# DMA transposes for three more attention units, earlier q and k for unit 1, and hidden-layer blocks laid around the last attn x v of batch 0

## Chip, cores, metric

One core of one Trainium2 chip. The metric is the device time of one execution in microseconds (us). Before the change it is 378.53 us (median of 3 runs, 378.49 to 378.64).

## The reference, cut to what matters

```python
# q, k, v: (8 batches, 12 heads, 448, 64) fp32; w_in (768, 2048), w_out (2048, 768)
scores = matmul(q, k.T) / 8
attn   = maximum(scores, 0) ** 2 / 448
x      = matmul(attn, v)             # laid out as (8 * 448, 768)
h      = x @ w_in
out    = maximum(h, 0) ** 2 @ w_out
```

The kernel works in fp16 with fp32 accumulation. It cuts the attention of a batch into three units of four heads, and a unit into seven tiles. Unit 0 has tiles 0 to 6, unit 1 has 7 to 13, and so on; batch 0 is units 0 to 2, batch 1 is units 3 to 5. A score matmul needs q and k with the head dimension on partitions, so each unit's q and k must be transposed first.

## The kernel before

There are two ways to get a transposed unit. Units 0 to 5 go the PE way (PE is TensorE, the matmul engine): whole-row loads (`load16`), 28 PE transposes into PSUM (the program's pools with `space=PSUM`), two copies out of PSUM. Units from 6 on go the DMA way: loads in pieces of 64 elements (`load_qk`), then two DMA transposes issued by SyncE (SP). All loads cast fp32 to fp16 and are issued by GpSimd (POOL).

```python
def load16(n):                        # whole rows: 2 x 448 elements a partition
    ...
    nc.gpsimd.dma_start(out=tq, in_=heads(q, n))
    nc.gpsimd.dma_start(out=tk, in_=heads(k, n))

def load_qk(n):                       # pieces of 64 elements (128 B in fp16)
    for src, nm in ((q, "qs"), (k, "ks")):
        t = blk_p.tile([P, J, 2, D], FP16, name=nm, tag=nm)
        for hh in range(2):
            nc.gpsimd.dma_start(out=t[:, :, hh, :], in_=...)

def dma_transpose(n):
    ts = new_qkt()
    for t, src in zip(ts, blks.pop(n)):
        nc.sync.dma_start_transpose(out=t, in_=src.rearrange("p j h d -> p (j h d)"))
    qkt[n] = ts
...
load16(0)
...
load_v(0); load16(1); load_v(1); load16(2); load_v(2)      # POOL's first loads
...
for i in range(11):                   # stage 1: batch 0's attention, tiles 0 to 20
    visit([t for t in (2 * i, 2 * i + 1) if t < NB0], turn={1: 1, 4: 2, 10: 3}.get(i))
    ...                               # loads of w_in and of units 3 to 5 between
load_v(6); load_w2(...) x 4; load_qk(6); load_qk(7)
# stage 2, "h stage": x @ w_in of batch 0 (16 groups of 6 matmuls), with batch 1's
# attention tiles and the PE transposes of units 4 and 5 woven in as "events";
# then x @ w_in of batch 1, where unit 6 (tile 42) starts at group 24
events.append((T_H + (1 + i // 2) * T_G, lambda i=i: sums_w2(i)))   # DVE sums of w_out blocks
events.append((T_H + (8 + i) * T_G, lambda i=i: sums_w1(i)))        # DVE sums of w_in blocks
```

The program gives each engine its instructions in a fixed order, and the traces show each waiting at the head of its own (below, PE stands still for 7.72 us before one score, with matmuls behind it that then wait for nothing). A small emission model (`at_pe`, `at_ve`: estimated times of PE and VectorE, DVE) decides where deferred DVE work is put in DVE's order:

```python
def av_unit():  ...; at_pe[0] += 2.65 ...                 # one attn x v of a unit
def visit(...): ...; at_pe[0] += 0.19 + 0.38 * len(tiles)
def fill(until):                      # puts deferred DVE work that the model thinks fits
    for d in (due, due_g):
        while d and max(at_ve[0], at_pe[0], d[0][0]) + d[0][1] <= until:
            put(d)
```

## Time and profile before

| | before |
|---|---|
| time, us | 378.53 |
| PE busy | 363.5 us, 96% |
| h stage of batch 0 begins in earnest | 30.22 us |
| tile 42 (unit 6) first scored | 71.05 us |
| q and k of unit 6 transposed by DMA | 65.95 us |

From the page of the kernel before: busy time per engine; the granted clock of PE, the DMA engines' busy share and what they moved, in 40 slices of the span; and the chain of work that ended last. PEld is PE's loading of weights, which overlaps PE. In the rows PEclk and DMA each digit is a slice in tenths; 9 is 90% or more.

```profile
PE 363.5 (96%) x3600; PEld 231.3 (61%) x3600; DVE 278.6 (74%) x515; ACT 249.8 (66%) x373; POOL 107.1 (28%) x128
PEclk9999999999999999999999999999999999999998
DMA  8999999999999999789498997893132200002333
GB/s 120 197 204 205 205 203 177 124 171 134 121 139 187 134 114 139 90 95 82 96 112 134 184 178 68 83 110 63 38 97 69 76 26 2 2 0 65 94 96 84
PE 81%; ACT 6%; DVE 6%; issue 2%; DMA 2%; POOL 1%; POOLq 0%; ACTq 0%; DVEq 0%
```

PE bounds the whole, but from the second slice to the sixth the loads run flat at 197 to 205 GB/s as well. What PE did, by the timeline (start, length, engine, line, operation, what was written and read, count, and the idle time before with what ended it):

```profile
11.49 0.58 PE L222 MATMUL slot<-ident,k 128*64 128x128 f16 x14 [0.72 <-DMA k<-in_k_dram]
...
30.22 2.81 PE L420 MATMUL mm<-xt,w 128*128 128x448 f16 x14 [0.25 <-ACT xt L280]
...
71.05 0.57 PE L252 MATMUL slot<-qT,kT 64*64 64x448 f16 x8
```

The transposes of unit 1's k waited 0.72 us for the load; tile 42 at 71.05 us waited for nothing. The DMA transposes of unit 6, by SP's timeline:

```profile
59.98 1.31 SPq L119 DMA_TRANSPOSE qT<-qs  x1
61.55 1.23 SPq L119 DMA_TRANSPOSE kT<-ks  x1
```

They landed 5.0 and 4.4 us after issue (the view of the tiles qT and kT), at 65.0 and 65.95 us, 5 us before tile 42. The wait of PE for squared attention tiles, by the waits view (total, times, longest, in us), is this:

```profile
PE slot L317 <- DVE at L369: 0.5, 2, 0.4
```

### The profile page before, as it was taken

Reading aid. Unit: us, or ns where it says so; the run is one execution under the profiler, and the core shown is the slowest. Engines: PE = TensorE matmul, PEld = TensorE weight load, DVE = VectorE, ACT = ScalarE, POOL = GpSimd, SP = SyncE. Lnnn points to the kernel's source line nnn. Section 1 sums busy time; section 2 is a strip of 40 time slices with the busy share of each in tenths; the row PEclk is TensorE's granted clock in tenths of the full one; section 3 lists DMA queues with packets and bytes.
Section 4 is the critical chain, followed back from the end, with each engine's and each line's share of the span. In section 5 each row is a group of like instructions: output and inputs, shape, how many; then the busy total and the mean of one; then the engine's idle time right before and its main releaser. Section 6 shows DMA issues by size and latency. Waiting matters only on the chain.

```text
span 377.6 us, 8806 instructions
## 1 busy us (share of the span) xinstructions
PE 363.5 (96%) x3600; PEld 231.3 (61%) x3600; DVE 278.6 (74%) x515; ACT 249.8 (66%) x373; POOL 107.1 (28%) x128
## 2 busy tenths in 40 slices
PE   7889999999999999999999999999999999999994
PEld 3544444444455678785555577877555588985663
DVE  1796567997767689897965758989956688995542
ACT  2897996686677798775566578877766785532220
POOL 8545431944440444404042243150000000000001
PEclk9999999999999999999999999999999999999998
DMA  8999999999999999789498997893132200002333
GB/s 120 197 204 205 205 203 177 124 171 134 121 139 187 134 114 139 90 95 82 96 112 134 184 178 68 83 110 63 38 97 69 76 26 2 2 0 65 94 96 84
DMA packets 121160, 42.65 MB, mean 113 GB/s; under 512 B 100832, under 2 KB 117760, under 8 KB 121120
## 3 DMA queue, kind: packets, MB, share of 16 engines
q0 software_dynamic: 82912, 23.01, 59.9%
q1 hardware_dynamic: 38048, 18.98, 26.2%
q8 instruction: 28, 0.46, 0.5%
q10 hardware_dynamic: 160, 0.10, 0.1%
q14 instruction: 12, 0.10, 0.1%
HBM read 45.61 MB, written 11.01 MB: 150 GB/s over the span
## 4 chain that ended last, share of the span: by engine, by line
PE 81%; ACT 6%; DVE 6%; issue 2%; DMA 2%; POOL 1%; POOLq 0%; ACTq 0%; DVEq 0%
PE mm L729 33%; PE mm L550 23%; PE slot L252 9%; PE mm L420 9%; PE slot L317 7%; ACT at L256 4%; DVE at L369 2%; DMA k<-in_k_dram 2%; PE slot L222 1%; DVE g L491 1%; ACT m L486 1%; DVE xt L283 1%; DVE s L602 1%; DVE g L498 0%; ACT qT L214 0%
## 5 line engine op out<-in xcount | busy, mean ns | idle before, releaser
L256 ACT ACTIVATE at<-slot 128x896 f16<-128x896 f32 x168 | 146.2, 920 | 33.0 <-PE slot L252 33.0
L369 DVE TENSOR_TENSOR at<-at 128x896 f16<-128x896 f16 x168 | 99.7, 618 | 15.7 <-ACT at L256 14.5
L108 POOL DMA_DIRECT2D qs<-in_q_dram x36 | 35.4, 984 | 121.3 <-DMA qT<-qs 113.6
L729 PEld LDWEIGHTS <-s 128*128 128x128 f16 x440 | 41.7, 98 | 32.0 <-issue 4.3
L252 PE MATMUL slot<-qT,kT 64*64 64x448 f16 x756 | 58.1, 360 | 2.6 <-ACT at L256 1.2
L550 PEld LDWEIGHTS <-w 128*128 128x128 f16 x576 | 54.4, 98 | 5.9 <-issue 5.4
L550 PE MATMUL mm<-xt,w 128*128 128x224 f16 x432 | 48.6, 259 | 0.0
L729 PEld LDWEIGHTS <-g 128*128 128x128 f16 x336 | 31.5, 98 | 24.0 <-issue 5.0
L550 PEld LDWEIGHTS <-ws 128*128 128x128 f16 x432 | 40.2, 98 | 6.7 <-issue 6.7
L729 PE MATMUL mm<-b,g 128*128 128x384 f16 x224 | 40.7, 326 | 0.0
L420 PE MATMUL mm<-xt,w 128*128 128x448 f16 x192 | 39.6, 353 | 0.3 <-ACT xt L280 0.3
L729 PE MATMUL mm<-b,s 128*128 128x384 f16 x216 | 39.6, 326 | 0.1
L729 PE MATMUL mm<-t,s 128*128 128x384 f16 x224 | 39.5, 326 | 0.0
L636 DVE SCALAR_TENSOR_TENSOR osb<-mm,u 128x384 f32<-128x384 f32 (+1 forms) x30 | 16.2, 541 | 31.2 <-ACT u L631 23.0
L252 PEld LDWEIGHTS <-kT 64*64 64x64 f16 x756 | 19.9, 104 | 31.1 <-issue 25.7
L108 POOL DMA_DIRECT2D ks<-in_k_dram x36 | 35.0, 975 | 9.9 <-DMA b<-in_moe_w_out_dram 5.8
L631 ACT ACTIVATE u<-mm 128x384 f32<-128x384 f32 x28 | 13.7, 491 | 32.6 <-PE mm L729 31.4
L571 POOL DMA_DIRECT2D out_dram<-osb x2 | 1.1, 563 | 120.5 <-DVE osb L636 120.5
L550 PE MATMUL mm<-x,ws 128*128 128x224 f16 x288 | 34.4, 259 | 0.9 <-ACT m L486 0.9
L317 PE MATMUL slot<-at,vt 64*64 64x448 f16 x588 | 32.2, 350 | 0.6 <-DVE at L369 0.5
L498 DVE TENSOR_TENSOR g<-g 128x896 f16<-128x896 f16 x48 | 29.7, 619 | 1.1 <-ACT g L501 0.2
L420 PEld LDWEIGHTS <-w 128*128 128x128 f16 x192 | 17.3, 98 | 19.1 <-issue 4.8
(66 smaller groups left out, 400.2 us busy)
## 6 DMA issues: line engine op xcount, KB each, us to landing
out_dram<-osb SPq DMA_DIRECT2D x52, 192.0 KB, 3.3
vt<-in_v_dram POOLq DMA_DIRECT2D x24, 224.0 KB, 6.6
qs<-in_q_dram POOLq DMA_DIRECT2D x36, 112.0 KB, 4.4
ks<-in_k_dram POOLq DMA_DIRECT2D x36, 112.0 KB, 5.3
w<-in_moe_w_in_dram POOLq DMA_DIRECT2D x8, 384.0 KB, 11.5
b<-in_moe_w_out_dram POOLq DMA_DIRECT2D x4, 768.0 KB, 17.1
q<-in_q_dram POOLq DMA_DIRECT2D x6, 224.0 KB, 8.3
k<-in_k_dram POOLq DMA_DIRECT2D x6, 224.0 KB, 8.6
```

Of the source, the lines that this page charges most:

```text
L108: nc.gpsimd.dma_start(out=t[:, :, hh, :], in_=heads(src, n)[:, hh].rearrange("p (j d) -> p j d", d=D))
L222: nc.tensor.transpose(pss[i][64 * hh:64 * hh + 64, i, j * P:(j + 1) * P], src[:, hh, j * D:(j + 1) * D], ident)
L252: nc.tensor.matmul(ps[c, hh, 0:S], lhsT=kT[r, j, c], rhs=qT[r, :, c], start=True, stop=True)
L256: nc.scalar.activation(out=at, in_=ps[:, :, 0:S], func=AF.Relu, scale=SK)
L317: nc.tensor.matmul(ps[64 * hh:64 * hh + 64, hp, 0:S], lhsT=vt[r, hh, j * D:(j + 1) * D], rhs=at[r, hh, :], start=(j == 0), stop=(j == J - 1))
L369: lambda: nc.vector.tensor_mul(at, at, at), 0))
L420: nc.tensor.matmul(cell[0][:, 0:S], lhsT=w1[f // 4][:, m, (f % 4) * P:(f % 4 + 1) * P], rhs=xts[b][:, m, :], start=(m == 0), stop=(m == NM ...
L498: due_g.append((t, 0.54, lambda: nc.vector.tensor_mul(g, g, g), b))
L550: nc.tensor.matmul(XY[s][y][:, r * Q:(r + 1) * Q], lhsT=left(k, i0 + 2 * s + r, m), rhs=right(k, m), start=(fresh and r == 0 and m == 0), ...
L631: nc.scalar.activation(out=t, in_=X[0][:, 0:HALF], func=AF.Copy, scale=CO)
L636: nc.vector.scalar_tensor_tensor(out=osb[row][:, c], in0=acc[0][:, 0:cc.stop - cc.start], scalar=CO, in1=keep[nm][:, cc], op0=ALU.mult, op ...
L729: nc.tensor.matmul(acc[0][:, 0:HALF], lhsT=left()[:, f], rhs=right[:, f], start=(fresh and f == 0), stop=(f == KH - 1), skip_group_check=n ...
```

## The change

Intent: give units 3 to 5 to the DMA way too, so that PE loses 84 transposes and ScalarE (ACT) loses the copies; load unit 1's q and k before unit 0's v; and fill PE's waits at the end of batch 0's attention with the first h blocks. The same diff moves three further things: tile 21 goes into stage 1, the weight sums on DVE move later, and two time constants of the emission model are halved. It also respaces the visits of the h stage and sets `reuse_waits` on one PSUM pool.

```diff
--- before.py
+++ after.py
@@ -157,11 +157,12 @@
     nc.vector.memset(zeros, 0.0)
     junk = const_p.tile([P, 1], FP16, name="junk", tag="junk")
     nc.scalar.activation(out=junk, in_=zeros[:, 0:1], func=AF.Relu)
+    load16(1)
     load_v(0)
-    load16(1)
+    load16(2)
     load_v(1)
-    load16(2)
     load_v(2)
+    load_qk(3)
 
     def sums_w1(i):
 
@@ -208,12 +209,9 @@
         ts = new_qkt()
         ps = slot(FP16)
 
-        def copy(i, eng):
-            dst = ts[i].rearrange("p j c -> p (j c)")
-            if eng == 0:
-                nc.scalar.activation(out=dst, in_=pss[i][:, i, 0:J * P], func=AF.Copy)
-            else:
-                nc.vector.tensor_copy(dst, pss[i][:, i, 0:J * P])
+        def copy(i):
+            nc.vector.tensor_copy(
+                ts[i].rearrange("p j c -> p (j c)"), pss[i][:, i, 0:J * P])
 
         pss = [ps, slot(FP16) if n == 0 else ps]
         for i, src in enumerate(srcs):
@@ -223,15 +221,12 @@
                         pss[i][64 * hh:64 * hh + 64, i, j * P:(j + 1) * P],
                         src[:, hh, j * D:(j + 1) * D], ident)
             if n == 0:
-                copy(i, 1)
+                copy(i)
                 warm(1)
         qkt[n] = ts
-        if n == 3:
-            return lambda: (copy(0, 0), copy(1, 0))
         if n > 0:
-            copy(0, n < 3)
-            copy(1, n < 3)
-        return None
+            copy(0)
+            copy(1)
 
 
     xts: dict = {}
@@ -305,7 +300,7 @@
             return
         unit[0] += 1
         flush(rest=False)
-        at_pe[0] += 2.65
+        at_pe[0] += 1.33
         b, u = divmod(n, NU)
         vt = vts[n]
         ps = slot(FP32)
@@ -379,17 +374,16 @@
             av_unit()
             for t in tiles[1:]:
                 score(t)
-            at_pe[0] += 0.19 + 0.38 * len(tiles)
+            at_pe[0] += 0.19 + 0.19 * len(tiles)
             for i, t in enumerate(tiles):
                 square(ats[t], 0.6 + 0.85 * i)
             return
         for t in tiles:
             score(t, 2)
-        later = pe_transpose(turn) if turn is not None else None
+        if turn is not None:
+            pe_transpose(turn)
         flush()
         av_some(lag, most)
-        if later:
-            later()
         for t in tiles:
             square(ats[t])
         flush()
@@ -774,21 +768,24 @@
     warm(10)
     pe_transpose(0)
     for i in range(11):
-        visit([t for t in (2 * i, 2 * i + 1) if t < NB0],
-              turn={1: 1, 4: 2, 10: 3}.get(i))
+        visit([2 * i, 2 * i + 1], turn={1: 1, 4: 2}.get(i))
         if i == 0:
-            load16(3)
             load_w1(0)
             load_w1(1)
+        if i == 2:
+            load_qk(4)
             load_v(3)
-        if i == 2:
-            load16(4)
             load_w1(2)
             load_v(4)
+        if i == 4:
+            dma_transpose(3)
         if i == 5:
-            load16(5)
+            load_qk(5)
             load_w1(3)
             load_v(5)
+        if i == 6:
+            dma_transpose(4)
+    dma_transpose(5)
     load_v(6)
     load_w2(b11, 0, 0)
     load_w2(b12, 0, 1)
@@ -797,17 +794,26 @@
     load_qk(6)
     load_qk(7)
     first.close()
-    big.append(ctx.enter_context(tc.tile_pool(name="mma", bufs=2, space=PSUM)))
-
-
-    f0 = h_group(0, 0)
-    for _, fn, _ in f0[0:4]:
-        fn()
+    big.append(ctx.enter_context(tc.tile_pool(
+        name="mma", bufs=2, space=PSUM, reuse_waits="tile")))
+
+
+
+    f0, f1 = h_group(0, 0), h_group(0, 1)
+
+    def some(part):
+        for _, fn, _ in part:
+            fn()
+
+    av_some(1, 9)
+    some(f0[0:2])
     av_some(0, 9)
     rounds.close()
     big.append(ctx.enter_context(tc.tile_pool(
         name="mmb", bufs=2, space=PSUM, side="right", reuse_waits="tile")))
-    visit([NB0, NB0 + 1])
+    some(f0[2:4])
+    some(f1[0:2])
+    visit([NB0 + 1, NB0 + 2])
 
     T_G = NM * 0.1892
     T_H = NF * T_G
@@ -816,14 +822,9 @@
     begin = [sum(T_O[:pr]) + 2 * (T_H + T_S * (pr - 1)) * (pr > 0) for pr in range(B // 2)]
 
     events = []
-    seq = [[2, 3], 4, [4, 5], [6, 7], [8, 9], 5, [10, 11], [12, 13], [14, 15],
-           [16, 17], [18, 19], [20], []]
-    for i, ts in enumerate(seq):
-        at = (2.5 + i) * T_G
-        if isinstance(ts, int):
-            events.append((at, lambda n=ts: pe_transpose(n)))
-        else:
-            events.append((at, lambda ts=ts: visit([NB0 + t for t in ts])))
+    for i in range(10):
+        ts = [NB0 + t for t in (2 * i + 3, 2 * i + 4)] if i < 9 else []
+        events.append(((1.5 + 1.46 * i) * T_G, lambda ts=ts: visit(ts)))
 
     def ready():
         early.close()
@@ -833,9 +834,9 @@
 
     events.append((T_H + 0.2, ready))
     for i in range(8):
-        events.append((T_H + (1 + i // 2) * T_G, lambda i=i: sums_w2(i)))
+        events.append((T_H + (4 + 0.75 * i) * T_G, lambda i=i: sums_w2(i)))
     for i in range(6):
-        events.append((T_H + (8 + i) * T_G, lambda i=i: sums_w1(i)))
+        events.append((T_H + (10 + 0.8 * i) * T_G, lambda i=i: sums_w1(i)))
     for i in range(2):
         events.append((2 * T_H + 3 + 3 * i, lambda i=i: sums_w1(6 + i)))
     for m in (6, 7):
@@ -875,8 +876,8 @@
     for i in (1, 2):
         events.append((2 * T_H - (3 - i) * T_G, lambda i=i: outs[0][1](i)))
 
-    steps = [(0.1892, None, False)] * 4 + f0[4:]
-    for f in range(1, NF):
+    steps = [(0.1892, None, False)] * 6 + f1[2:4] + f0[4:6] + f1[4:6]
+    for f in range(2, NF):
         steps += h_group(0, f)
     for f in range(NF):
         steps += h_group(1, f)
```

## The prediction

> **What bounds it now.** By the page, PE is busy 96% and the chain that ended last is 81% PE. By stage, the first 72 us differ. By the timeline, batch 0's hidden product (mm, L420) starts in earnest at 30.22 us and ends about 62.0; the same PE work without gaps (86 matmuls of 0.191, 21 scores of 0.25, three attn x v of 1.32, two transposes of 0.92) sums to 27.7, so some 3.5 us are bubbles, behind ACT (4.3 to 4.8 of 5 us busy in the windows from 35 to 60), which also does four 0.92 us copies of transposed q and k there. The loads are bound too: from 12 to 56 us nearly every 1 us window moves 200 to 215 GB/s on one software queue. The q and k of unit 6, late in that queue, land by 61.5; its transposed k lands at 65.95 (issue 61.55 + 4.4); PE first uses it at 71.12. Slack: 5.2 us.
>
> **What the change does.** Removed: 84 PE transposes (2.8 us of PE), six ACT copies (5 us). One batch-1 tile moves into the first stage with doubled scores (+0.25 us PE). Unit 1's k lands about 1.15 us earlier, against a 0.87 us idle of ACT. First-stage end: perhaps 1.5 to 2 us earlier, its waits filled by h blocks. On PE and ACT alone, tile 42 (unit 6, group 24 of the h stage) would start 6 to 7.5 us earlier.
>
> Added: loads of units 3 to 5 in 128 B pieces. Such loads ran at 153 to 161 GB/s at 57 to 60 us against 205: +0.38 us per 224 KB, six times: +2.3 us. Six DMA transposes: the Trainium skill, "DMA: Bandwidth & Descriptors" (Latency and other measured facts), gives 261 GB/s; this trace shows 254 and 297 in the two windows at 64 to 66 us that hold little else, so 0.77 to 0.88 us each: +4.6 to 5.3 us. The same page (Issuing engines are not separate DMA queues) says all queues share 16 DMA engines; at 60 to 62 us the total stayed at 155, so I add both to a saturated queue.
>
> Hence unit 6's transposed k lands near 65.95 + 7 to 7.6 = 73 to 73.6, after 71.12. PE is in order there and later work is unchanged. Units 4 and 5 should stall PE earlier too (estimated 2 to 4 us each).
>
> **Sum.** End = 377.6 - 71.12 + start of tile 42. At 73.3: +2.2 us, less 0.5 to 1 because DVE catches up (PE waits 0.5 us at 94 and 0.7 at 122 now). That gives about 380. If transposes overlap loads better than I think, the gain is up to 6 us. Point 379.4, range 374.5 to 382.5; faster by over 2% 0.05, within 2% 0.92, slower 0.03.
>
> **What would show it.** PE busy falls by about 3 us. The DMA row stays at 9 or more until about 70 us, not 63. DMA transposes of units 4 and 5 land in 5 to 7 us while loads run. PE waits on kT or qT before scores of tiles 28, 35 and 42. Tile 42's first score starts at 72 to 75 us. From there to the end both traces take the same time within 1 us. The h stage starts about 28.5 us.
>
> **What would make it wrong.** Transposes using DMA time that loads leave free, so that unit 6 lands by 68 and PE's gain survives (372 to 374). Or transposes starved by loads (over 7 us each), w_in blocks late, and PE stalls over 3 us that lower its clock (382 and more).

## The result, and the profile after

The changed kernel takes 399.91 us (median of 4 runs, 399.23 to 400.44) against 378.56 (median of 4). The ratio is 1.0563, 95% interval 1.0545 to 1.0581: slower by 5.6%. Ratios here and below are the mean time of one kernel's fast runs over the mean of the other's of the same rounds, so they are not quite the ratio of the medians quoted.

From the page of the changed kernel, the same lines:

```profile
PE 366.7 (92%) x3520; PEld 230.6 (58%) x3520; DVE 279.9 (70%) x515; ACT 245.3 (62%) x367; POOL 114.9 (29%) x134
PEclk9986997999899999999999999999999999999998
DMA  8999999999989999998959999949032230000333
GB/s 117 184 167 179 167 176 204 154 144 137 145 85 170 184 123 132 90 110 73 92 127 131 126 176 134 93 62 117 10 64 65 80 81 2 2 2 18 104 97 100
PE 70%; DVE 11%; DMA 10%; ACT 5%; issue 2%; POOLq 0%; POOL 0%; ACTq 0%; DVEq 0%
```

PE lost 80 matmuls (84 transposes went, 4 doubled scores came), yet it is busy 3 us longer, and in three of the first seven slices its granted clock is below 9 tenths. PE's share of the chain fell from 81 to 70%; DMA and DVE took it. PE's timeline shows where it stood still:

```profile
31.90 0.96 PE L247 MATMUL slot<-qT,kT 64*64 64x448 f16 x8 [6.64 <-DMA kT<-ks]
...
44.57 0.38 PE L247 MATMUL slot<-qT,kT 64*64 64x448 f16 x4 [0.48 <-DMA kT<-ks]
...
60.64 0.59 PE L247 MATMUL slot<-qT,kT 64*64 64x448 f16 x4 [7.72 <-DMA kT<-ks]
...
85.06 0.57 PE L247 MATMUL slot<-qT,kT 64*64 64x448 f16 x8
...
101.07 0.38 PE L312 MATMUL slot<-at,vt 64*64 64x448 f16 x4 [2.98 <-DVE at L364]
```

PE waited 6.64 us before tile 21, 0.48 before tile 28 and 7.72 before tile 35 (the first tiles of units 3, 4 and 5), each time for kT from a DMA transpose. Together that is 14.84 us. Tile 42 starts at 85.06 us, 14.0 later than before. From there to the end of the span the kernel before took 377.6 - 71.05 = 306.6 us and the changed one 398.1 - 85.06 = 313.0. So the loss has two parts, 14.0 us before unit 6 and 6.5 us after it. By the waits view over the whole span:

```profile
PE slot L247 <- DMA kT<-ks: 14.8, 3, 7.7
PE slot L312 <- DVE at L364: 5.1, 4, 3.0
```

The second line answers to the one of before: DVE now delays PE by 5.1 us in place of 0.5. SP's timeline shows when the transposes of units 3 to 5 were issued:

```profile
18.23 1.33 SPq L119 DMA_TRANSPOSE qT<-qs  x1
20.72 3.84 SPq L119 DMA_TRANSPOSE kT<-ks  x1
32.62 1.22 SPq L119 DMA_TRANSPOSE qT<-qs  x1
34.14 3.72 SPq L119 DMA_TRANSPOSE kT<-ks  x1
45.13 1.22 SPq L119 DMA_TRANSPOSE qT<-qs  x1
47.02 3.70 SPq L119 DMA_TRANSPOSE kT<-ks  x1
```

The second number is SP's own time for one issue: 3.7 to 3.8 us for each kT, against 1.2 for unit 6 in the kernel before. The view of tile kT shows when the last of these landed, for which PE waited 7.72 us:

```profile
L119 SPq DMA_TRANSPOSE kT<-ks x1: 3700/3700/3700, 47.0 to 47.0; - x1
DMA to landing us min/median/max: 13.6/13.6/13.6
```

The six took 9.5 to 13.6 us (q: 11.0, 9.5, 10.4; k: 11.1, 10.4, 13.6), two to three times the 4.4 to 5.0 of unit 6 before. And PE's clock, by the windows view (span, its length; then busy us and count for PE, PEld, DVE, ACT, POOL; then PEclk, DMA share, GB/s):

```profile
core 0: us, PE busy (x) PEld busy (x) DVE busy (x) ACT busy (x) POOL busy (x), PEclk, DMA share, GB/s
25.00:30.00 5.00, 0.26 (x6) 0.00 (x0) 2.06 (x4) 1.58 (x2) 1.31 (x3) 0.73 1.58 137
30.00:35.00 5.00, 3.10 (x26) 1.04 (x26) 0.62 (x1) 0.92 (x1) 2.91 (x4) 0.50 2.26 162
55.00:60.00 5.00, 0.00 (x0) 0.00 (x0) 0.00 (x0) 0.00 (x0) 0.60 (x2) 0.80 1.30 183
60.00:65.00 5.00, 4.36 (x15) 1.73 (x16) 1.38 (x3) 0.92 (x1) 1.85 (x2) 0.52 1.32 204
```

In and after the two long waits the clock is 0.50 to 0.80. Four matmuls of 448 columns after the first wait took 1.68 us, where six take 1.31 at full clock. After the second wait 12 matmuls took 4.23 us in place of 2.44; no later wait before tile 42 hides these 1.8 us. The fall of the clock in the long waits agrees with the Trainium skill, "TensorE: Matmul & The Clock Gate" (Part 1: The HAM clock gate), which says that an idle window of about 3.4 us puts PE back to half clock.

### The profile page after: what moved, and what is told of

Same layout as the page of the kernel before. It is cut to its first block, busy times and chain, and to the rows that moved or that the text cites. A ratio compares the mean times of both kernels' runs of the same rounds, so it can differ in the third digit from the quotient of the medians.

```text
span 398.1 us, 8659 instructions
## 1 busy us (share of the span) xinstructions
PE 366.7 (92%) x3520; PEld 230.6 (58%) x3520; DVE 279.9 (70%) x515; ACT 245.3 (62%) x367; POOL 114.9 (29%) x134
## 4 chain that ended last, share of the span: by engine, by line
PE 70%; DVE 11%; DMA 10%; ACT 5%; issue 2%; POOLq 0%; POOL 0%; ACTq 0%; DVEq 0%
PE mm L723 30%; PE mm L544 22%; DMA kT<-ks 9%; PE slot L247 8%; PE slot L312 6%; ACT at L251 4%; PE mm L414 4%; DVE at L364 3%; DVE s L596 1%; DVE g L492 1%; DMA q<-in_q_dram 1%; DVE t L151 1%; ACT m L480 1%; PE slot L220 1%; DVE osb L630 1%
## 5 line engine op out<-in xcount | busy, mean ns | idle before, releaser
L108 POOL DMA_DIRECT2D qs<-in_q_dram x42 | 41.4, 988 | 129.6 <-DMA qT<-qs 118.4
L247 PE MATMUL slot<-qT,kT 64*64 64x448 f16 x760 | 59.0, 364 | 17.0 <-DMA kT<-ks 14.8
L108 POOL DMA_DIRECT2D ks<-in_k_dram x42 | 41.0, 977 | 12.2 <-DMA b<-in_moe_w_out_dram 5.8
L723 PE MATMUL mm<-b,g 128*128 128x384 f16 x224 | 42.4, 336 | 0.0
L414 PE MATMUL mm<-xt,w 128*128 128x448 f16 x192 | 42.2, 372 | 0.0
L723 PE MATMUL mm<-b,s 128*128 128x384 f16 x216 | 39.6, 326 | 0.1
```

Of the source, the lines that this page charges most:

```text
L108: nc.gpsimd.dma_start(out=t[:, :, hh, :], in_=heads(src, n)[:, hh].rearrange("p (j d) -> p j d", d=D))
L247: nc.tensor.matmul(ps[c, hh, 0:S], lhsT=kT[r, j, c], rhs=qT[r, :, c], start=True, stop=True)
L414: nc.tensor.matmul(cell[0][:, 0:S], lhsT=w1[f // 4][:, m, (f % 4) * P:(f % 4 + 1) * P], rhs=xts[b][:, m, :], start=(m == 0), stop=(m == NM ...
L723: nc.tensor.matmul(acc[0][:, 0:HALF], lhsT=left()[:, f], rhs=right[:, f], start=(fresh and f == 0), stop=(f == KH - 1), skip_group_check=n ...
```

## The experiments

All kernels gave correct results. "Before" medians of the four groups of runs were 378.87, 378.86, 379.3 and 378.73 us. Except for `k_first`, each experiment starts from the changed kernel or from a named variant of it.

### 1. PE transposes again, everything else kept: `pe_turns`

```diff
-    load_qk(3)                          # and 4, 5
+    load16(3)                           # and 4, 5, at the same places of POOL's order
-        visit([2 * i, 2 * i + 1], turn={1: 1, 4: 2}.get(i))
+        visit([2 * i, 2 * i + 1], turn={1: 1, 4: 2, 9: 3}.get(i))
-            dma_transpose(3)            # and 4, 5
+    events.append((3.7 * T_G, lambda: pe_transpose(4)))
+    events.append((6.6 * T_G, lambda: pe_transpose(5)))
```

> The changed kernel, but units 3 to 5 are loaded in whole rows and transposed on PE again (copies on DVE); everything else of the change stays. Theory T (the DMA transposes are what costs: 14.8 us of PE stalls before scores of tiles 21, 28 and 35, and the cold clock behind them): the stalls before tiles 21, 28, 35 vanish, tile 42 starts at 66 to 70 us against 85.06, and the time is 378 to 384 (above the PE gain because a DVE delay of some 3 us near the end of the h stage and one of some 3 us near 290 stay). Rival L (the other parts of the change cost it: reordered loads, h blocks, DVE order): still over 390.

Measured: 385.11 us (383.19 to 387.71), ratio 1.0164 (1.0115 to 1.0213). All PE waits for kT of a DMA transpose are gone, by the waits view, and batch 1's part of the h stage begins at 61.31 us (60.73 before, 74.74 in the changed kernel):

```profile
61.31 10.39 PE L413 MATMUL mm<-xt,w 128*128 128x448 f16 x54
71.63 0.57 PE L246 MATMUL slot<-qT,kT 64*64 64x448 f16 x8
```

Tile 42 starts at 71.63 us, not at the 66 to 70 that I had expected. The one wait of 2.98 us for DVE stayed. The scatter follows the granted clock: the run of 383.19 had a mean of 1.000, the profiled one of 387.71 had 0.984, with a clock of 0.50 from 87 to 93 us, behind that wait. The time ends a little above what I expected, but rival L falls: the DMA way for units 3 to 5 is some 15 us of the 21.

### 2. Small pieces loaded, PE transposes: `pieces_pe`

```diff
-        srcs = q16s.pop(n)
+        srcs = q16s.pop(n) if n < 3 else [t.rearrange("p j h d -> p h j d") for t in blks.pop(n)]
# otherwise as pe_turns, with load_qk kept; loads of unit 5, 6 and 7 placed after
# the PE transposes that free their buffers
```

> As pe_turns, but q and k of units 3 to 5 are loaded in 128 B pieces, as in the changed kernel, and transposed on PE from there. Theory T: the pieces alone lengthen the load queue by about 2.3 us and the time by 0 to 2 us over pe_turns. Rival P (the small pieces are what starves the rest): at least half of the 21 us loss is back, over 389.

Measured: 383.24 us (383.05 to 384.49), ratio 1.0117 (1.0092 to 1.0142). Rival P falls. The pieces do lengthen the load queue: SP could issue the transpose of unit 7's k, which waits for the last of these loads, at 68.53 us in place of 65.00 in `pe_turns`, so 3.5 us, waits of POOL for free buffers included, and not the 2.3 that I had estimated. But no wait of PE in this run is for a load. I had expected 0 to 2 us more than `pe_turns`; the median is 1.9 us less. The clock accounts for it: the runs at a mean of 1.000 took 383.05 and 383.22 here, and 383.19 there.

### 3. PE kept busy through the waits: `held_clock`

```diff
         for t in tiles:
+            if t == NB0:            # tile 21
+                warm(32)
             score(t, 2)
...
             for t in tiles[1:]:
+                if t == 5 * J:      # tile 35
+                    warm(38)
                 score(t)
```

> The changed kernel with 32 dummy matmuls of 448 columns put between the scores of tiles 20 and 21 and 38 between those of 34 and 35, where PE waits 6.6 and 7.7 us for transposed k. They do no useful work and fit into the waits. Theory C (PE's clock, 0.50 to 0.75 in the windows from 30 to 40 and 0.52 from 60 to 65, costs 4 to 5 us on top of the stalls): granted clock stays at 1.0 until 100 us and the time falls to 394 to 397. Rival: the lower clock lies in time that PE has to spare and nothing changes (399 to 401), or it rises if dummies delay the scores.

Measured: 400.16 us (398.64 to 402.52), ratio 1.0543 (1.0509 to 1.0578): no gain. PE's timeline shows why:

```profile
25.52 6.21 PE L204 MATMUL slot<-zeros 128*128 128x448 f16 x32 [0.57 <-ACT at L251]
...
46.77 0.59 PE L247 MATMUL slot<-qT,kT 64*64 64x448 f16 x4 [5.44 <-DMA kT<-ks]
```

The dummies covered the first wait and the clock stayed at 1.0 until 40 us. PE then reached tile 28 at 41.3 us, 2.8 sooner, and waited there 5.44 us, not 0.48, until kT of unit 4 had landed; in that wait its clock fell to 0.50. So what the clock costs after the first wait is spent in front of the next wait and is not a term of its own: theory C falls there. For the second wait this run decides nothing: kT of unit 5 landed at 62.3 us, but the dummies ran on and held tile 35 back to 64.00.

### 4. Transposes on an empty queue: `gated`

```diff
+    def hold(n):
+        for i in range(2):
+            nc.gpsimd.tensor_copy(held[:, i:i + 1], qkt[n][i][:, 0, 0:1])
+            dma_transpose(3)
+            hold(3)                  # POOL issues no load until both have landed
             load_w1(0)           # these stood before the transposes
             load_w1(1)
             load_qk(4)
# the same behind dma_transpose(4) and dma_transpose(5)
```

> The changed kernel, but GpSimd, which issues all loads, first reads one column of the transposed q and k of units 3, 4 and 5 before it issues the loads behind them, so each pair of DMA transposes runs on a queue that has run dry. Theory Q (each transposing DMA takes 9.5 to 13.6 us because loads on the other queue share its engines): transposes of units 3 to 5 land 3.5 to 6 us after issue, the stall before tile 21 shrinks from 6.6 us to under 1.5; the loads come some 10 us later instead, so the whole is 385 to 405. Rival S (the transposes themselves are slow when two follow each other at that place): 9 us and more even here.

Measured: 407.75 us (407.45 to 408.13), ratio 1.0757 (1.0735 to 1.0779). The whole is slower, as loads now come late: PE waits 10.00 us before tile 42, 3.57 before tile 35, and 3.3 and 4.2 us for w_in and v. The total is above my range, and all landings but one are below theirs. But the question was the landing time, by the view of tile kT:

```profile
L119 SPq DMA_TRANSPOSE kT<-ks x3: 1221/1230/1232, 19.5 to 56.5; - x3
DMA to landing us min/median/max: 2.9/2.9/3.0
```

The three of k landed in 2.9 to 3.0 us and those of q in 3.0 to 3.7, where the changed kernel shows 9.5 to 13.6. The wait before tile 21 was gone. So these transposes are slow because of the loads beside them; rival S falls. The windows view of the first pair, with nothing else in flight (the last number is GB/s):

```profile
19.00:20.00 1.00, 0.84 (x18) 0.57 (x19) 1.00 (x3) 1.00 (x2) 0.00 (x0) 1.00 0.63 126
20.00:21.00 1.00, 1.00 (x29) 0.73 (x21) 1.00 (x3) 0.73 (x2) 0.00 (x0) 1.00 0.80 152
21.00:22.00 1.00, 1.00 (x23) 0.56 (x19) 0.96 (x2) 1.00 (x2) 0.19 (x1) 1.00 0.94 181
```

126 + 152 + 181 = 459 KB in 3 us is the size of the pair, 153 GB/s on average. SP issued the two 1.4 us apart and the engines' share was only 0.63 to 0.94, so the pace may be that of the issues; how fast the engines could go is not measured here.

### 5. Half the dose: `q_only_dma`

```diff
+    def dma_transpose_q(n):
+        ts = new_qkt()
+        src = blks[n].pop(0)
+        nc.sync.dma_start_transpose(out=ts[0], in_=src.rearrange("p j h d -> p (j h d)"))
+        qkt[n] = ts
# pieces_pe, with this for q of units 3 to 5; PE transposes k only
```

> As pieces_pe, but q of units 3 to 5 goes through DMA transposes and k through PE: half the dose. Theory R (transposes and loads take turns packet by packet on the shared engines, so a transpose under load needs about 3 us plus a time that grows with the number of transposes queued): a single one lands in 6 to 8 us, against 9.5 to 11 (q) and 10.4 to 13.6 (k) for pairs; PE's waits for qT stay under 3 us in all; time 383 to 389. Rival B (a transpose under load is slow by a fixed delay, queued or not): 9.5 to 11 us again and stalls of 3 to 6 us each, over 389.

Measured: 389.38 us (387.75 to 390.15), ratio 1.0253 (1.0211 to 1.0294). The landing time of the first, by the view of tile qT:

```profile
L126 SPq DMA_TRANSPOSE qT<-qs x1: 1310/1310/1310, 17.7 to 17.7; - x1
DMA to landing us min/median/max: 10.8/10.8/10.8
```

The other two took 9.5 and 10.8 us. One transpose of q alone under load is as slow as that of a pair (9.5 to 11.0), so theory R, my picture of packets taking turns, falls in the form in which I put it, though PE's waits for qT were 4.0 us in all and the time was just over the line. The cost to the load queue does go with the number: SP issued unit 7's kT at 68.53 us with no added transpose (`pieces_pe`), at 73.49 with three and at 79.31 with six. That is 1.65 and 1.8 us each, where the prediction had 0.77 to 0.88. Gaps in the flow of loads are included, in which POOL waited for buffers or PE stood still, so this is the delay of the loads and not the engine time of a transpose.

### 6. A short line of loads: `shallow`, `shallow_old_both`

```diff
+    def room(cost, rows, ap):       # before each load, from w_in on
+        while flight and sum(f[0] for f in flight) > 4.0:
+            _, r, a = flight.popleft()
+            nc.gpsimd.tensor_copy(held[r, c:c + 1], a)   # waits for the oldest load
+        flight.append((cost, rows, ap))
```

> The changed kernel, but from the loads of w_in on GpSimd issues a load only when the loads still in flight are worth at most 4 us of the queue's time (it reads one column of the oldest first); before, eight loads (up to 15 us and more) were in flight. The loads keep flowing, only the line behind them is short. Theory F (a DMA transpose lands only after the loads that were already issued when it was issued, which is why one or two transposes take the same 10 us): transposes of units 3 to 5 land 5 to 7.5 us after issue, PE's waits for transposed k fall from 14.8 us to under 7, GB/s stays mostly at 190 to 205, time 385 to 393. Rival R (packet-by-packet sharing with a busy load queue, whatever its depth): 9 us and more again, time 397 to 402.

> shallow with the old places of the weight sums and the old time constants. If these are apart from the transposes, 4 to 6 us less than shallow: 380 to 388. Only if transposes land in time everywhere would it beat the kernel before (378.6).

In the changed kernel the landing times suggested a line: a w_in load issued at 16.99 us landed after 12.2 us, at 29.2, and qT issued at 18.23 landed at 29.2 as well. `shallow` took 407.68 us (405.37 to 410.82), ratio 1.0775 (1.0732 to 1.0818), and the two fast runs of `shallow_old_both` 401.83 and 403.91, ratio 1.0621; its other two, the profiled one among them, are slow, so I read nothing from its trace. Both totals are above every range that I had given. In `shallow` the transposes of q took 9.4, 6.3 and 7.1 us and those of k 13.7, 8.5 and 8.7, and PE's waits for kT were 20.8 us in all. Neither theory holds: five of the six are shorter than in the changed kernel, but only two are within the 5 to 7.5 us that theory F gave, and k of unit 3 took longer. With a pair and w_in loads in flight the engines at times moved little: 80 and 81 GB/s in the windows from 22 to 24 us of this run. In the changed kernel the windows view shows when, with the pair of unit 3 in flight from 18.23 and 20.72 us on:

```profile
20.00:21.00 1.00, 1.00 (x31) 0.76 (x23) 1.00 (x3) 0.73 (x2) 0.72 (x2) 1.00 1.27 214
28.00:29.00 1.00, 0.00 (x0) 0.00 (x0) 0.00 (x0) 0.00 (x0) 0.00 (x0) 0.50 1.81 72
```

From 18 to 26 us each window moves 183 to 214 GB/s, about what loads alone move; from 26 to 32, when the two land (29.2 and 31.8), only 72 to 161. So the slow stretch is the end of the flight and not the whole of it. The view does not say whose bytes moved when. `shallow` also let the queue run dry later (PE waited 7.03 us before tile 42), so its total says little.

### 7. The moved weight sums and the time constants

The 6.5 us after unit 6 could not come from transposes of units 3 to 5. Two parts of the diff reach that far: the place of the weight sums, and the constants of the emission model. Each was undone on `pieces_pe`:

```diff
# pieces_pe_old_sums
-        events.append((T_H + (4 + 0.75 * i) * T_G, lambda i=i: sums_w2(i)))
+        events.append((T_H + (1 + i // 2) * T_G, lambda i=i: sums_w2(i)))
-        events.append((T_H + (10 + 0.8 * i) * T_G, lambda i=i: sums_w1(i)))
+        events.append((T_H + (8 + i) * T_G, lambda i=i: sums_w1(i)))
# pieces_pe_old_clock
-        at_pe[0] += 1.33
+        at_pe[0] += 2.65
-            at_pe[0] += 0.19 + 0.19 * len(tiles)
+            at_pe[0] += 0.19 + 0.38 * len(tiles)
# pieces_pe_old_both: both
```

> pieces_pe with the sums of weights on DVE placed as before the change (from one group after the end of batch 0's h stage on, not four; those of w_in from group 8, not 10). Theory V (the later place packs DVE so full that the last attn x v of the h stage waits 2.98 us for a squared tile): that wait falls below 0.5 us and the time falls by 3 to 5 us from pieces_pe (383.2), the part over 3 being clock. Rival W (the wait comes from the changed time constants): wait and time stay.

> pieces_pe with the old time constants of the emission model (2.65 us for an attn x v, 0.38 per score), which decide where deferred DVE work is put in DVE's order. Theory: the DVE-led stall near 270 to 280 us (some 2.5 us) goes and the time falls by 2 to 3 us; the wait of 2.98 us at the end of the h stage stays. Rival W: it is this that removes the 2.98 us.

> pieces_pe with both, so what is left of the change is the load order, the pieces, DVE for all copies of transposed tiles, the moved tile and the h blocks around the attn x v. If the two act apart, the gains add: 376 to 378.5, that is at or below the kernel before (378.6). If they overlap or the moved h blocks cost something, 379 to 381.

Measured: old sums 380.13 us (379.74 to 380.97), ratio 1.0018 (0.998 to 1.0056); old constants 382.0 (381.21 to 382.88), ratio 1.0065 (1.0024 to 1.0105); both 378.56 (378.02 to 382.41), ratio 0.9995 (0.9951 to 1.004). The waits view of PE for squared tiles in `pieces_pe` has the same line as in the changed kernel (5.1, 4, 3.0). With old sums, then with old constants, it is:

```profile
PE slot L312 <- DVE at L364: 2.2, 3, 1.6
```

```profile
PE slot L312 <- DVE at L364: 3.5, 3, 3.0
```

Old sums remove the wait of 2.98 us at the end of the h stage; old constants remove one of 1.65 us near 277 us. With both undone 0.5 us of such waits are left, as before the change, so the waits are apart. The gains in time agree with adding up (3.1 and 1.2 us of medians singly, 4.7 together; by the ratios 3.7, 2.0 and 4.6), but the intervals, some 1.5 us each way, would not show a small overlap. I had expected 2 to 3 us of the constants. Rival W falls.

> The changed kernel, DMA transposes and all, with the old places of the weight sums and the old time constants. Theory A (their cost is apart from the transposes): the same 4 to 5 us as on pieces_pe go, 394.5 to 396.5, and the waits of 2.98 us (h stage end) and 1.65 us (near 294) go. Rival: with the later loads of w_out the old places make DVE wait for them, and the time stays at 398 to 401.

The same two undone on the changed kernel itself, DMA transposes kept (`after_old_both`): 393.46 us (392.76 to 394.34), ratio 1.0381 (1.0349 to 1.0413), so 6.45 us of medians less than the changed kernel, somewhat more than expected. The wait line of its span, and tile 42 in its timeline:

```profile
PE slot L312 <- DVE at L364: 0.5, 2, 0.4
```

```profile
85.68 0.57 PE L247 MATMUL slot<-qT,kT 64*64 64x448 f16 x8
```

The waits are those of the kernel before. Tile 42 starts at 85.68 us and the span ends at 392.1: 306.4 us, where the kernel before takes 306.6. In the changed kernel the wait of 2.98 us was followed by a clock of 0.74 from 100 to 105 us; 16 matmuls there took 4.45 us in place of 2.77. The waits (5.1 less 0.5) and these 1.7 us make 6.3 of the 6.45. But the same wait left the clock at 1.00 in `pieces_pe`, and no run separates what decides it.

### 8. What is worth keeping: `k_first`, `best1`

```diff
# k_first: the kernel before, only this
+    load16(1)
     load_v(0)
-    load16(1)
+    load16(2)
     load_v(1)
-    load16(2)
     load_v(2)
# best1: pe_turns with old sums and old constants, and
-    events.append((3.7 * T_G, lambda: pe_transpose(4)))
+    events.append((2.3 * T_G, lambda: pe_transpose(4)))
```

> The kernel before with only the first loads reordered: q and k of unit 1 ahead of v of unit 0. k of unit 1 lands about 1.2 us earlier and PE's wait of 0.72 us for it goes; ACT bounds most of the rest of that stage, so 0.3 to 1 us less: 377.6 to 378.3.

> The candidate: load order, moved tile and h blocks of the change; whole-row loads and PE transposes for units 3 to 5, copied by DVE; unit 4 turned one and a half groups earlier than in pe_turns (there a score waited 1.24 us for DVE's copy); old time constants and old places of the weight sums. Expected h stage end 1 to 2 us earlier than before and no DVE stall: 376 to 378; not below 375.

Measured: `k_first` 378.16 us (377.99 to 378.61), ratio 0.9971 (0.9956 to 0.9987); `best1` 377.98 (377.8 to 378.77), ratio 0.9968 (0.9952 to 0.9984). Both are within 2% of the kernel before; the intervals put them 0.1 to 0.5% below it, and the two cannot be told apart. PE's wait for unit 1's k is gone in `k_first`, as expected. Tile 42 starts at 69.96 us in `k_first` and at 69.70 in `best1`. The h blocks, the moved tile and the copies on DVE add nothing that is measurable here.

## Why the prediction was wrong

- **The result.** I forecast 379.4 us, 374.5 to 382.5; it is 399.91. The warning at the end ("transposes starved by loads (over 7 us each) ... PE stalls over 3 us") describes what happened, but I had not put it into the range.
- **The step that failed first: "DMA transposes of units 4 and 5 land in 5 to 7 us while loads run."** They landed in 9.5 to 13.6 us, and unit 3's, which I left out of the list of stalls altogether, in 11.0 and 11.1. I had taken the landing time from unit 6 of the kernel before, whose loads were nearly over. `gated` shows 2.9 to 3.7 us without loads, and `pe_turns` shows that without these transposes the stalls go. An estimate from the issue times above: had each kT landed 7 us after its issue, PE would have waited 2.5 us at tile 21, not at all at tile 28 and 1.1 at tile 35, in place of 6.64, 0.48 and 7.72.
- **"0.77 to 0.88 us each."** I read this from two windows in which bytes of several transposes were booked at once, and the Trainium skill, "DMA: Bandwidth & Descriptors" (Latency and other measured facts), with its 261 GB/s seemed to agree. Neither says what a transpose costs beside loads: there each put off the end of the loads by 1.65 to 1.8 us, gaps included (`q_only_dma` and the changed kernel against `pieces_pe`). As an estimate of that delay the term was half of what was measured. No run here tests the 261 GB/s itself.
- **Unit 6 as the place where it is decided.** The sum ran from the arrival of unit 6 alone. Tile 42 did start late, at 85.06 us, but PE did not wait there: the 14.84 us were lost before tiles 21, 28 and 35. Units 4 and 5 were named as stalls of "2 to 4 us each", but the sum has no term for them; unit 5's alone was 7.72. In-order stalls add up where each is longer than the slack behind it.
- **"Later work is unchanged."** Wrong, by 6.5 us. The diff has two edits that move DVE work for the rest of the span, and I read them as bookkeeping. `after_old_both` shows that with them undone the rest takes 306.4 us, as before.
- **"PE busy falls by about 3 us."** It rose from 363.5 to 366.7, since half the clock makes matmuls longer: by the pages, the 192 of the first h stage took 42.2 us in place of 39.6. Count matmuls, not busy time, where the clock differs.
- **Right:** loads and transposes do hold each other up, as the same page leads one to expect (Issuing engines are not separate DMA queues: all run on the same 16 engines). In the changed kernel the last loads came 14.5 us later, by SP's issue of unit 7's kT, and in `gated` the transposes alone were fast. Unit 1's k no longer made PE wait.
- **Not tested:** that PE and ACT alone would bring tile 42 "6 to 7.5 us earlier". No run has the shorter PE work without the late transposes; `best1`, which keeps the PE transposes, gains 1.35 us there.

The sum closes as follows, by ratios to the kernel before. With DMA transposes, the moved sums and the constants it is 1.0563; without the sums and constants 1.0381; without the transposes as well 0.9995. So 1.8% are the sums and constants, 3.9% the DMA transposes with the stalls that they cause, and the rest of the change comes to nothing within the interval (0.9951 to 1.004).

**Open:** why a transpose beside loads is so slow. The skill's page (Queues, rings and completion order) says that each engine takes turns between its queues packet by packet, and that a completion mark lands only after every earlier write of that engine across its queues. No run here shows the first. Landing times that follow the order of issue fit the second, but `shallow` did not bring the times that a line of loads would give, and stretches of 72 to 81 GB/s with both in flight, where loads alone move some 200 and a pair alone 153, are not explained by a line either.

## What to carry to other kernels

Work taken from a busy engine and given to DMA engines that loads already keep busy is not free: measure the landing time of such a transfer beside the load that it will meet, not in a quiet stretch, and compare it with the slack of the first instruction that needs it. In a program whose engines run in order, one late transfer stops all work behind it; here PE also came back from the waits of 6.64 and 7.72 us with a clock of 0.50. Read every edit of a diff for how far it reaches: here the new places of some sums and two constants of a scheduling model cost 6 us in stages that the change did not mean to touch.

## What the Trainium skill lacked or had wrong

- "DMA: Bandwidth & Descriptors" gives a bandwidth for DMA transposes (261 GB/s), but nothing of their latency beside other loads: here 128 x 896 fp16 took 2.9 to 3.7 us with no load beside it and 9.5 to 13.6 us beside a saturated load queue (q 9.5 to 11.0, whether alone or with k behind it). The 261 GB/s was not reached by a pair on the empty queue (153 GB/s, at a DMA share below 1), and it is not refuted.
- The same page says that a transpose next to ordinary DMAs needs nothing. That holds for correctness here (all runs were correct); for speed it lacks that a transpose beside loads landed three times as late, and that stretches with both in flight moved as little as 72 GB/s, against about 200 for the loads alone.
- "TensorE: Matmul & The Clock Gate" (Part 1) names an idle window of about 3.4 us as what brings back half clock. The waits of 6.64 and 7.72 us agree in that both brought it (clock 0.50), though in the first the clock fell about 2 us after PE's last matmul. Shorter waits did it too: by 1 us windows the clock fell to 0.50 after the wait of 2.98 us in the changed kernel and in `pe_turns`, and after 2.50 and 2.72 us in `q_only_dma`, in three of these four only when PE was already running again. After the same 2.98 us in `pieces_pe` it stayed at 1.00. What decides is not shown; 3.4 us is not a safe limit here.
